# A later decay, a bonus term inside its own step, and weights prepared in the third step: another issue order for an RWKV-6 plus maxout kernel

## The chip, the cores and the metric

The kernel runs on one core of a Trainium2 chip. The metric is device time in microseconds (us) from start to end of one execution; less is better. Besides the timed runs there is one profiled execution, from which all rows below are taken. The engines are named as in the profile: PE (TensorE matmul), PEld (its weight loads), DVE (VectorE), ACT (ScalarE), POOL (GpSimd), and SPq, the queue of SyncE, which in this kernel issues every DMA.

## The reference

Two blocks follow each other. The first is a linear attention with a decaying state, for 4 batches, 8 heads, 768 tokens and a head dimension of 48:

```
state = 0
for t in range(768):
    y[t]  = r[t] @ (state + (u * k[t]) outer v[t])      # the u part is the "bonus" term
    state = w[t][:, None] * state + k[t] outer v[t]     # w is the decay, 0.8 to 0.95
```

The second is a feed-forward block on the 3072 rows of y, each of 8 x 48 = 384 numbers:

```
out = maximum(x @ w1, x @ w2) @ w_out                   # 384 -> 1024 -> 384
```

## The kernel before

**Units.** A unit is one chunk of 128 tokens of two batches; there are NU = 12, and unit n has the state g = n % 2. Inside a chunk the decay is turned into cumulative products, so that the recurrence becomes matmuls: scores inside the chunk (`scores`, `y_intra`), the part from the state (`y_inter`), and the update of the state (`kv`, `decay`). The maximum is computed as half of (sum + |difference|): |x (w1 - w2)| goes through `gate`, and x (w1 + w2) w_out / 2 through a 384 x 384 matrix `wc_sb` that `weights` prepares once: it needs the sums `ws_sb`, their 24 transpositions, 24 matmuls with `wo_sb`.

**Steps.** Step n of a software pipeline handles three units: its own unit a = n (log, cumulative sum, exponentials, scaled r and k), unit t = n - 1 (transpositions, scores, state, y) and unit m = n - 2 (feed-forward, output). There are 14 steps. The order in which every engine gets its instructions is the order of the program text (a manual schedule): an engine whose next instruction waits does nothing else, and SPq neither. So the sequence written in the main loop (L369 to L397) is the sequence on each engine.

**The decay's way.** `exps` (L203) computes the cumulative log decay `mz` of a unit. Its last row is needed on partitions, one value for each head and dimension. So it goes through DRAM: two DMAs write it to `row` (L212), two more read it back into `WL` (L216), which waits on SPq until the first have landed. `decay_exp` (L238, on ACT) makes `Wt` out of it one step later, `decay` (L264, on POOL) multiplies the state with it.

**The bonus.** `bonus_mul` (L171, POOL) casts v to bf16 (`vb`) and forms r * k * u (`rku`, two multiplications); `bonus_sum` (L181) sums it on DVE (`dg`) and multiplies v with that on POOL (`vd`). In step n they are issued for unit n + 1.

**DMAs.** On SPq a step holds, in this order: the 8 loads of unit n + 2, `row` of unit n, `WL` of unit n, and the two outputs of unit n - 2 (192 KB each, L363). An output's tile `osb` is one of three.

**PSUM.** The tag "tr" (transpositions) has one buffer, "go" (gates, outputs, wc) two, "y" one, "sc" one.

Of the kernel before, what the change touches and what calls it, by code (L numbers as in the profile page):

```python
# [8 lines left out]
F32 = mybir.dt.float32  # L9
# [25 lines left out]
def _body(tc, r, k, v, w, u, moe_w1, moe_w2, moe_w_out, out):  # L35
    nc = tc.nc
    B, H, S, D = r.shape
    P = 128
# [3 lines left out]
    HD = H * D  # L42
# [5 lines left out]
    NU = NC * B // 2  # L48
# [9 lines left out]
    def wt_(shape, dt, tag, bufs=None):  # L58
        return wk.tile(shape, dt, tag=tag, name=tag, bufs=bufs)

    def pt_(shape, dt, tag, bufs=1):
        return ps.tile(shape, dt, tag=tag, name=tag, bufs=bufs)

    def unit(n):
        return n // 2, (n % 2) * 2
# [5 lines left out]
    def load(n):  # L71
        c, b0 = unit(n)
        d = {}
        for name, src in (("w", w), ("k", k), ("r", r), ("v", v)):
            t = ldp.tile([P, H, 2, D], F32, tag="l" + name, name="l" + name)
            for b in range(2):
                nc.sync.dma_start(  # L77
                    out=t[b * Q:(b + 1) * Q].rearrange("p h i d -> p h (i d)"),
                    in_=src[b0 + b, :, c * C:(c + 1) * C, :].rearrange(
                        "h (p i) d -> p h (i d)", i=2))  # L80
            d[name] = t
        L[n] = d
# [5 lines left out]
    w1f = const.tile([P, KO, d_ff], F32)  # L88
    w2f = const.tile([P, KO, d_ff], F32)
# [29 lines left out]
    for i in range(NRK):  # L119
        t = const.tile([P, 2, 2, H, DP], BF16, name=f"rkn{i}")  # L120
# [14 lines left out]
    ws_sb = const.tile([P, KO, d_ff], BF16)  # L135
# [4 lines left out]
    def weights():  # L140
        for ko in range(KO):
            nc.vector.tensor_sub(wd_sb[:, ko, :], w1f[:, ko, :], w2f[:, ko, :])
            nc.gpsimd.tensor_add(ws_sb[:, ko, :], w1f[:, ko, :], w2f[:, ko, :])  # L143
        nc.scalar.mul(wo_sb, wof, 0.5)
        for ko in range(KO):
            tp = pt_([P, FO, P], BF16, "tr")
            for fo in range(FO):
                nc.tensor.transpose(tp[:, fo, :], ws_sb[:, ko, fo * P:(fo + 1) * P], ident)  # L148
            nc.vector.tensor_copy(
                wsT_sb.rearrange("p f (k c) -> p k f c", k=KO)[:, ko, :, :], tp)  # L150
        for ko in range(KO):
            wc_p = pt_([P, HD], F32, "go", 2)
            for fo in range(FO):
                nc.tensor.matmul(wc_p, wsT_sb[:, fo, ko * P:(ko + 1) * P],
                                 wo_sb[:, fo, :], start=(fo == 0), stop=(fo == FO - 1))
            nc.scalar.copy(wc_sb[:, ko, :], wc_p)


    U = {}

    def byi(t):
        return t.rearrange("p h i d -> p i h d")

    def logw(n):
        s = U[n] = {}
        s["lw"] = lw = wt_([P, H, 2, D], F32, "lw")
        nc.scalar.activation(lw, L[n]["w"], AF.Ln)  # L167
        s["lp"] = lp = wt_([P, H, D], F32, "lp")
        nc.gpsimd.tensor_add(lp, lw[:, :, 0, :], lw[:, :, 1, :])  # L169

    def bonus_mul(n):  # L171
        s = U[n]
        s["vb"] = vb = wt_([P, H, 2, D], BF16, "vb", 3)
        nc.gpsimd.tensor_copy(vb, L[n]["v"])
        s["rku"] = rku = wt_([P, H, 2, D], F32, "rku", 1)
        nc.gpsimd.tensor_mul(rku, L[n]["r"], L[n]["k"])  # L176
        nc.gpsimd.tensor_mul(  # L177
            byi(rku), byi(rku),
            u_b.rearrange("p (h d) -> p h d", h=H).unsqueeze(1).to_broadcast([P, 2, H, D]))

    def bonus_sum(n):  # L181
        s = U[n]
        dg = wt_([P, H, 2, 1], F32, "dg")
        nc.vector.reduce_sum(dg, s["rku"], axis=AX.X)  # L184
        s["vd"] = vd = wt_([P, 2, H, D], BF16, "vd", 3)
        nc.gpsimd.tensor_mul(byi_inv(vd), L[n]["v"], dg.to_broadcast([P, H, 2, D]))  # L186

    def byi_inv(t):
        return t.rearrange("p i h d -> p h i d")
# [13 lines left out]
    def exps(n):  # L203
        s = U[n]
        mz = s["mz"]
        nc.scalar.activation(s["A"][:, 1].rearrange("p h d -> p (h d)"), mz[:, 0], AF.Exp)
        s["iA"] = iA = wt_([P, 2, H, D], F32, "iA", 1)
        nc.scalar.activation(iA.rearrange("p i h d -> p i (h d)"), mz, AF.Exp, scale=-1.0)
        row = drp.tile([2, HD], F32, tag="row", name="row")
        for b in range(2):  # L210
            e = (b + 1) * Q
            nc.sync.dma_start(out=row[b:b + 1, :], in_=mz[e - 1:e, 1, :])  # L212
        s["WL"] = wl = WL[n % 2]
        rowv = row.rearrange("b (p r d) -> r d (b p)", r=2, d=D)
        for par in range(2):
            nc.sync.dma_start(  # L216
                out=wl[par * DP:par * DP + D, :, :].rearrange("d b p -> d (b p)"),
                in_=rowv[par])

    def scale_rk(n):  # L220
        s = U[n]
        s["rkn"] = rkn = rkn_b[n % NRK]
        nc.vector.tensor_mul(rkn[:, 0, :, :, 0:D], byi(L[n]["r"]), s["A"])
        nc.vector.tensor_mul(rkn[:, 1, :, :, 0:D], byi(L[n]["k"]), s["iA"])  # L224
# [39 lines left out]
    def decay(n):  # L264
        c, b0 = unit(n)
        if c == NC - 1:
            return
        g = b0 // 2
        nc.gpsimd.tensor_mul(S_f[g], T_f[g], U[n]["Wt"].to_broadcast([P, 2, NP, D]))  # L269
        for e in range(2):  # L270
            q = slice(e * DP, (e + 1) * DP)
            nc.gpsimd.tensor_copy(S_b[g][q, :, :, e * D:(e + 1) * D], S_f[g][q])  # L272
# [52 lines left out]
    def xt(n):  # L325
        s = U[n]
        tp = pt_([P, KO, 2, P], BF16, "tr")
        for b in range(2):
            for ko in range(KO):
                nc.tensor.transpose(tp[:, ko, b, :], s["x"][:, b, ko * P:(ko + 1) * P], ident)  # L330
        s["xT"] = xT = wt_([P, KO, 2, P], BF16, "xT")
        nc.scalar.copy(xT, tp)  # L332

    def gate(n, j):
        s = U[n]
        if j == 0:
            s["gT"] = wt_([P, FO, 2, P], BF16, "gT")
        g = pt_([P, 2, 2 * P], F32, "go", 2)
        for f in range(2):
            fo = 2 * j + f  # L340
            for ko in range(KO):
                nc.tensor.matmul(g[:, f, :], wd_sb[:, ko, fo * P:(fo + 1) * P],  # L342
                                 s["xT"][:, ko].rearrange("p j t -> p (j t)"),
                                 start=(f == 0 and ko == 0), stop=(f == 1 and ko == KO - 1),
                                 skip_group_check=True)
        nc.scalar.activation(s["gT"][:, 2 * j:2 * j + 2].rearrange("p f j t -> p f (j t)"), g,  # L346
                             AF.Abs)

    def outp(n, b):
        c, b0 = unit(n)  # L350
        s = U[n]
        o = pt_([P, HD], F32, "go", 2)
        for ko in range(KO):
            nc.tensor.matmul(o, s["xT"][:, ko, b, :], wc_sb[:, ko, :],  # L354
                             start=(ko == 0), stop=False)
        for fo in range(FO):
            nc.tensor.matmul(o, s["gT"][:, fo, b, :], wo_sb[:, fo, :],  # L357
                             start=False, stop=(fo == FO - 1))
        osb = wt_([P, HD], F32, "osb", 3)
        nc.scalar.copy(osb, o)  # L360
        tok = (b0 + b) * S + c * C
        dst = out[tok:tok + C, :].rearrange("(q i) n -> i q n", i=2)
        nc.sync.dma_start(out=dst, in_=osb)  # L363


    logw(0)
    bonus_mul(0)
    bonus_sum(0)
    for n in range(NU + 2):  # L369
        a, t, m = n, n - 1, n - 2  # L370
        A, T, M = a < NU, 0 <= t < NU, 0 <= m < NU
        if n >= 1 and n + 2 < NU:
            load(n + 2)
        if n == 1:
            weights()
        if T: transp(t, 0)
        if A: cumsum(a)
        if M: gate(m, 0)
        if T: transp(t, 1)
        if A: exps(a)  # L380
        if M: gate(m, 1)
        if T: kv(t)
        if T: scores(t, 0)
        if a + 1 < NU: logw(a + 1)
        if M: gate(m, 2)
        if M: gate(m, 3)
        if T: decay_exp(t)
        if T: scores(t, 1)
        if T: y_inter(t)
        if T: decay(t)  # L390
        if a + 1 < NU: bonus_mul(a + 1)
        if A: scale_rk(a)
        if M: outp(m, 0)
        if T: y_intra(t)
        if a + 1 < NU: bonus_sum(a + 1)
        if M: outp(m, 1)
        if T: xt(t)  # L397

    ps.release()
    drp.release()  # L400
# [33 lines left out]
```

## Time and profile before

| | |
|---|---|
| median of 3 runs | 253.65 us (251.24 to 253.86) |
| profiled execution, its own time | 251.43 us |
| its span on the core | 249.6 us |
| PE busy | 154.7 us (62%) |
| POOL busy | 122.2 us (49%) |
| DVE busy | 109.4 us (44%) |
| ACT busy | 92.0 us (37%) |
| loads of one unit | 8 DMAs of 192 KB |
| outputs of one unit | 2 DMAs of 192 KB |

The span is from the first to the last instruction of the core; the own time has 1.8 us more around it. No engine is busy for much over half of the span, so the time has to be read from waits. The profile offers these views for it: a chain of work that ended last, with start and length of each piece; a list of who waited for whom; a timeline of single instructions; groups of instructions by line; and windows, which give for a stretch the busy time of each engine, the granted clock of PE (1.00 is 2.4 GHz, 0.50 is 1.2 GHz), the busy share of the 16 DMA engines and what they moved.

### The profile page before, as it was taken

What the parts mean: (1) busy time and instruction counts of PE and PEld (TensorE: products, weight loads), DVE (VectorE), ACT (ScalarE), POOL (GpSimd) and SP (SyncE); (2) the same over time, 40 slices, a digit from 0 to 9 for tenths busy, and PEclk for the clock granted to TensorE, in tenths of its full rate; (3) what the DMA queues carried; (4) which work ended last, traced back from release to release, by engine and by line L of the source; (5) the groups of instructions that cost most, each with busy time, mean ns of one, the idle gap of its engine ahead of it and who ended that gap; (6) DMA issues with size and microseconds to landing.
All of it is one profiled execution on the core that took longest, in us unless ns stands there. A gap on an engine that the chain in (4) does not pass through costs nothing.

```text
span 249.6 us, 5117 instructions
## 1 busy us (share of the span) xinstructions
PE 154.7 (62%) x2104; PEld 104.0 (42%) x2104; DVE 109.4 (44%) x132; ACT 92.0 (37%) x161; POOL 122.2 (49%) x119
## 2 busy tenths in 40 slices
PE   0200039568869696977729819919809919989820
PEld 0000025445556464645426417507507606666510
DVE  5042781667557482828416406507406605632000
ACT  3021041526445464647126125235134234534510
POOL 7378890294968868594183192192193166000000
PEclk9999999858999999999968976997986995999995
DMA  6999995969147138247148138237337311111110
GB/s 134 208 208 390 373 201 88 198 109 149 12 127 175 17 103 188 34 131 172 17 112 188 18 103 183 31 100 179 41 98 172 49 42 25 46 26 50 50 50 36
DMA packets 65463, 28.91 MB, mean 116 GB/s; under 512 B 60424, under 2 KB 64672, under 8 KB 65440
## 3 DMA queue, kind: packets, MB, share of 16 engines
q1 hardware_dynamic: 65440, 28.59, 52.2%
q8 instruction: 16, 0.26, 0.4%
q14 instruction: 7, 0.06, 0.1%
HBM read 23.83 MB, written 4.76 MB: 115 GB/s over the span
## 4 chain that ended last, share of the span: by engine, by line
DMA 27%; PE 23%; POOL 19%; issue 11%; ACT 6%; SPq 5%; DVE 5%; DVEq 0%; POOLq 0%; ACTq 0%
DMA out_dram<-osb 13%; DMA row<-mz 9%; PE go L342 7%; PE tr L231 5%; POOL rku L176 5%; POOL rku L177 4%; POOL ws_sb L143 4%; PE go L357 3%; PE ex L195 3%; POOL Sb L272 3%; DMA u_b<-in_u_dram 2%; SPq L77 2%; ACT xT L332 2%; DVE rT L236 2%; SPq L216 2%
## 5 line engine op out<-in xcount | busy, mean ns | idle before, releaser
L184 DVE TENSOR_REDUCE dg<-rku 128x16 f32<-128x768 f32 x12 | 11.4, 953 | 86.7 <-POOL rku L177 86.7
L342 PE MATMUL go<-xT,wd_sb 128*128 128x256 bf16 x288 | 41.7, 293 | 1.0 <-ACT xT L332 1.0
L231 PE MATMUL tr<-ident,rkn 128*128 128x128 bf16 x192 | 18.3, 251 | 34.9 <-ACT xT L332 27.4
L357 PE MATMUL go<-wo_sb,gT 128*128 128x384 bf16 x192 | 35.1, 326 | 0.0
L342 PEld LDWEIGHTS <-wd_sb 128*128 128x128 bf16 x288 | 29.1, 106 | 12.5 <-issue 7.0
L286 DVE TENSOR_TENSOR M<-sc,mask 128x1024 bf16<-128x1024 f32 x24 | 29.3, 1221 | 7.9 <-PE sc L283 7.9
L231 PEld LDWEIGHTS <-rkn 128*128 128x128 bf16 x192 | 15.9, 114 | 38.9 <-issue 38.0
L169 POOL TENSOR_TENSOR lp<-lw 128x384 f32<-128x384 f32 x12 | 12.4, 1037 | 39.1 <-ACT lw L167 39.1
L346 ACT ACTIVATE gT<-go 128x512 bf16<-128x512 f32 x48 | 27.7, 593 | 10.2 <-PE go L342 9.9
L360 ACT COPY osb<-go 128x384 f32<-128x384 f32 x24 | 11.4, 474 | 41.3 <-PE go L357 19.5
L357 PEld LDWEIGHTS <-gT 128*128 128x128 bf16 x192 | 18.8, 98 | 12.4
L186 POOL TENSOR_TENSOR vd<-lv,dg 128x768 bf16<-128x768 f32 x12 | 17.7, 1474 | 12.8 <-DVE dg L184 12.8
L269 POOL TENSOR_TENSOR Sf<-Tf,Wt 128x384 f32<-128x384 f32 x10 | 8.3, 828 | 29.5 <-ACT Wt L241 28.5
L176 POOL TENSOR_TENSOR rku<-lr,lk 128x768 f32<-128x768 f32 x12 | 22.3, 1855 | 0.0
L177 POOL TENSOR_TENSOR rku<-rku,u_b 128x768 f32<-128x768 f32 x12 | 21.7, 1806 | 0.9
L195 PE MATMUL ex<-lp,tri 128*128 128x384 f32 x24 | 15.5, 741 | 7.5 <-POOL lp L169 7.5
L148 PE MATMUL tr<-ident,ws_sb 128*128 128x128 bf16 x24 | 3.1, 307 | 26.8 <-POOL ws_sb L143 22.1
L272 POOL CAST Sb<-Sf 64x384 bf16<-64x384 f32 x20 | 15.5, 776 | 1.1
L354 PE MATMUL go<-wc_sb,xT 128*128 128x384 bf16 x72 | 15.7, 328 | 0.0
L199 ACT ACTIVATE A<-ex 128x384 f32<-128x384 f32 x12 | 5.9, 490 | 24.1 <-PE ex L195 24.1
L148 PEld LDWEIGHTS <-ws_sb 128*128 128x128 bf16 x24 | 2.5, 138 | 28.3 <-POOL ws_sb L143 26.6
L224 DVE TENSOR_TENSOR rkn<-lk,iA 128x768 bf16<-128x768 f32 x12 | 13.3, 1104 | 0.0
(55 smaller groups left out, 225.8 us busy)
## 6 DMA issues: line engine op xcount, KB each, us to landing
lw<-in_w_dram SPq DMA_DIRECT2D x24, 192.0 KB
lk<-in_k_dram SPq DMA_DIRECT2D x24, 192.0 KB
lr<-in_r_dram SPq DMA_DIRECT2D x24, 192.0 KB
lv<-in_v_dram SPq DMA_DIRECT2D x24, 192.0 KB
out_dram<-osb SPq DMA_DIRECT2D x24, 192.0 KB
w1f<-in_moe_w_dram SPq DMA_DIRECT2D x1, 1536.0 KB
w2f<-in_moe_w_dram SPq DMA_DIRECT2D x1, 1536.0 KB
wof<-in_moe_w_out_dram SPq DMA_DIRECT2D x1, 1536.0 KB
```

Source lines behind the costliest of these rows:

```text
L176: nc.gpsimd.tensor_mul(rku, L[n]["r"], L[n]["k"])
L177: nc.gpsimd.tensor_mul(byi(rku), byi(rku), u_b.rearrange("p (h d) -> p h d", h=H).unsqueeze(1).to_broadcast([P, 2, H, D]))
L186: nc.gpsimd.tensor_mul(byi_inv(vd), L[n]["v"], dg.to_broadcast([P, H, 2, D]))
L195: nc.tensor.matmul(ex, tri2, lp.rearrange("p h d -> p (h d)"))
L224: nc.vector.tensor_mul(rkn[:, 1, :, :, 0:D], byi(L[n]["k"]), s["iA"])
L231: nc.tensor.transpose(tp[:, p, :, i, :], s["rkn"][:, x, i, 2 * p:2 * p + 2, :].rearrange("s r d -> s (r d)"), ident)
L272: nc.gpsimd.tensor_copy(S_b[g][q, :, :, e * D:(e + 1) * D], S_f[g][q])
L286: nc.vector.tensor_mul(M.rearrange("s e p t -> s (e p) t"), sc.rearrange("s e p t -> s (e p) t"), mask[:, i].rearrange("s i q -> s (i q)") ...
L342: nc.tensor.matmul(g[:, f, :], wd_sb[:, ko, fo * P:(fo + 1) * P], s["xT"][:, ko].rearrange("p j t -> p (j t)"), start=(f == 0 and ko == 0) ...
L346: nc.scalar.activation(s["gT"][:, 2 * j:2 * j + 2].rearrange("p f j t -> p f (j t)"), g, AF.Abs)
L354: nc.tensor.matmul(o, s["xT"][:, ko, b, :], wc_sb[:, ko, :], start=(ko == 0), stop=False)
L357: nc.tensor.matmul(o, s["gT"][:, fo, b, :], wo_sb[:, fo, :], start=False, stop=(fo == FO - 1))
```

## The change

`exps` only sends `row` off; reading it back into `WL` becomes a function of its own, `decay_load`, issued for unit t = n - 1 at the very start of step n, ahead of that step's loads. `decay` of a unit moves from the middle of its own step to the start of the next one. `bonus_mul` and `bonus_sum` of unit a are issued in step a itself, after its exponentials and after its scaling. `osb` gets 6 buffers. `weights` moves from step 1 to step 2, between the work of unit 1 and the rest of the step, and its three sums move from POOL to DVE.

```
@@ weights
-            nc.gpsimd.tensor_add(ws_sb[:, ko, :], w1f[:, ko, :], w2f[:, ko, :])
+            nc.vector.tensor_add(ws_sb[:, ko, :], w1f[:, ko, :], w2f[:, ko, :])
@@ exps
             nc.sync.dma_start(out=row[b:b + 1, :], in_=mz[e - 1:e, 1, :])
+        s["row"] = row
+
+    def decay_load(n):
+        s = U[n]
+        row = s["row"]
         s["WL"] = wl = WL[n % 2]
         rowv = row.rearrange("b (p r d) -> r d (b p)", r=2, d=D)
         for par in range(2):
...
@@ outp
-        osb = wt_([P, HD], F32, "osb", 3)
+        osb = wt_([P, HD], F32, "osb", 6)
@@ main loop
-    logw(0)
-    bonus_mul(0)
-    bonus_sum(0)
-    for n in range(NU + 2):
...
-        if n == 1:
-            weights()
...
+    def step(a, t, m):
+        A, T, M = a is not None, t is not None, m is not None
+        if T and t >= 1: decay(t - 1)
         if T: transp(t, 0)
         if A: cumsum(a)
         if M: gate(m, 0)
         if T: transp(t, 1)
         if A: exps(a)
+        if A: bonus_mul(a)
         if M: gate(m, 1)
         if T: kv(t)
         if T: scores(t, 0)
-        if a + 1 < NU: logw(a + 1)
+        if A and a + 1 < NU: logw(a + 1)
         if M: gate(m, 2)
         if M: gate(m, 3)
         if T: decay_exp(t)
         if T: scores(t, 1)
         if T: y_inter(t)
-        if T: decay(t)
-        if a + 1 < NU: bonus_mul(a + 1)
         if A: scale_rk(a)
+        if A: bonus_sum(a)
         if M: outp(m, 0)
         if T: y_intra(t)
-        if a + 1 < NU: bonus_sum(a + 1)
         if M: outp(m, 1)
         if T: xt(t)
+
+    logw(0)
+    for n in range(NU + 2):
...
+        if t is not None:
+            decay_load(t)
+        if n >= 1 and n + 2 < NU:
+            load(n + 2)
+        if n == 2:
+            step(None, t, None)
+            weights()
+            step(a, None, m)
+        else:
+            step(a, t, m)
```

## Rows read from the trace of the kernel before

**Rows 1.** The page's first line.

```profile
span 249.6 us, 5117 instructions
```

**Rows 2.** Waits of SPq: who waited for what: us in total, times, longest.

```profile
SPq L216 <- DMA row<-mz: 50.5, 12, 7.2
```

**Rows 3.** The chain that ended last, two cycles: start us, length us, what.

```profile
122.16 6.57 DMA out_dram<-osb
...
141.23 6.56 DMA out_dram<-osb
```

**Rows 4.** Timeline, 134 to 143 us: start us, length us, engine, line, operation [idle before].

```profile
135.13 1.06 SPq L212 DMA_DIRECT2D row<-mz  x2
140.30 0.84 SPq L216 DMA_DIRECT2D WL<-row  x2
...
142.81 0.21 ACT L241 ACTIVATE Wt<-WL 128x8 f32<-128x8 f32 x1 [5.15 <-DMA WL<-row]
```

**Rows 5.** Windows of 1 us; the last three columns: PE clock, DMA share, GB/s.

```profile
127.00:128.00 1.00, 0.00 (x0) 0.00 (x0) 0.00 (x0) 0.00 (x0) 1.00 (x1) 0.50 0.13 49
140.00:141.00 1.00, 1.00 (x37) 0.77 (x37) 0.40 (x1) 0.00 (x0) 0.00 (x0) 1.00 0.00 0
141.00:142.00 1.00, 1.00 (x8) 0.61 (x7) 0.00 (x0) 0.00 (x0) 0.00 (x0) 1.00 0.29 2
236.00:237.00 1.00, 1.00 (x8) 0.61 (x7) 0.00 (x0) 0.00 (x0) 0.00 (x0) 1.00 0.14 51
```

**Rows 6.** Waits of the engines over the whole span.

```profile
DVE dg L184 <- POOL rku L177: 86.7, 12, 11.2
...
ACT osb L360 <- DMA out_dram<-osb: 19.4, 6, 3.9
```

**Rows 7.** Timeline of the start, 35 to 70 us.

```profile
35.44 0.68 DVE L149 COPY wsT_sb<-tr 128x1024 bf16<-128x1024 bf16 x1
...
39.76 0.84 SPq L216 DMA_DIRECT2D WL<-row  x2
...
43.95 0.61 PE L231 MATMUL tr<-ident,rkn 128*128 128x128 bf16 x8
...
49.94 1.23 DVE L286 TENSOR_TENSOR M<-sc,mask 128x1024 bf16<-128x1024 f32 x1 [0.74 <-PE sc L283]
...
51.76 0.80 ACT L323 CAST x<-y 128x768 bf16<-128x768 f32 x1 [3.15 <-PE y L318]
...
54.33 1.01 PE L231 MATMUL tr<-ident,rkn 128*128 128x128 bf16 x8 [0.89 <-ACT xT L332]
...
68.82 0.61 PE L231 MATMUL tr<-ident,rkn 128*128 128x128 bf16 x8 [0.93 <-ACT xT L332]
```

**Rows 8.** Groups by line: busy us, mean ns of one, idle before and releaser.

```profile
L286 DVE TENSOR_TENSOR M<-sc,mask 128x1024 bf16<-128x1024 f32 x24 | 29.3, 1221 | 7.9 <-PE sc L283 7.9
...
L208 ACT ACTIVATE iA<-mz 128x768 f32<-128x768 f32 x12 | 10.1, 840 | 0.0
L167 ACT ACTIVATE lw<-lw 128x768 f32<-128x768 f32 x12 | 10.0, 835 | 3.4 <-DMA lw<-in_w_dram 3.4
...
L142 DVE TENSOR_TENSOR wd_sb<-w1f,w2f 128x1024 bf16<-128x1024 f32 x3 | 8.1, 2741 | 1.1 <-DMA w2f<-in_moe_w_dram 1.1
...
L206 ACT ACTIVATE A<-mz 128x384 f32<-128x384 f32 x12 | 6.2, 520 | 14.7 <-DVE mz L200 14.7
```

**Rows 9.** The chain that ended last, from step 11 on.

```profile
206.41 1.01 PE tr L231 x8
...
220.77 0.62 PE tr L231 x8
...
232.11 1.47 PE go L342 x12
...
238.93 0.48 ACT osb L360
```

**Rows 10.** Timeline of step 11: the first output copy of the step.

```profile
217.09 0.48 ACT L360 COPY osb<-go 128x384 f32<-128x384 f32 x1 [2.32 <-PE go L357]
```

More of the change, by code (lines that the diff above doesn't have):

```diff
@@ L363, in outp @@
         nc.sync.dma_start(out=dst, in_=osb)
-    logw(0)
-    bonus_mul(0)
-    bonus_sum(0)
-    for n in range(NU + 2):
[L370 to L373, printed above, removed]
-        if n == 1:
-            weights()
+    def step(a, t, m):
+        A, T, M = a is not None, t is not None, m is not None
+        if T and t >= 1: decay(t - 1)
         if T: transp(t, 0)
@@ L389, in _body @@
         if T: y_inter(t)
-        if T: decay(t)
-        if a + 1 < NU: bonus_mul(a + 1)
         if A: scale_rk(a)
+        if A: bonus_sum(a)
         if M: outp(m, 0)
         if T: y_intra(t)
-        if a + 1 < NU: bonus_sum(a + 1)
         if M: outp(m, 1)
         if T: xt(t)
+    logw(0)
+    for n in range(NU + 2):
+        a = n if n < NU else None
+        t = n - 1 if 0 <= n - 1 < NU else None
+        m = n - 2 if 0 <= n - 2 < NU else None
+        if t is not None:
[8 more added lines that the diff above has]
+            step(a, t, m)
     ps.release()
```

## The prediction

> **What bounds the kernel now.** I read the page's first line (the span, 249.6 us [rows 1]), then the waits of SPq, then the chain, then windows of 1 us where the chain sits on DMAs.
>
> SPq, in order, spends 50.5 us in 12 waits for `row` to land before it may read `WL` back [rows 2]. The chain repeats a cycle of 141.23 - 122.16 = 19.07 us from output to output [rows 3]. SPq fills it without a gap: outputs from 122.16, loads, `row` at 135.13, a wait until 140.30, `WL` [rows 4], outputs at 141.23.
>
> What are the DMA engines doing in it? In 127 to 128, outputs alone move 49 GB/s at a share of 0.13, in the tail 51 GB/s at 0.14 [rows 5]: 0.13 x 16 is about two engines of 16. So an output of 196,608 bytes takes 196,608 / 50 GB/s = 3.93 us and a pair 7.86 us on those two. One output is 6.57 us from issue to landing [rows 3]; I split the other 2.6 us evenly: 1.3 us before the first byte, 1.3 us until the landing is seen. Loads and `row` go to the same engines behind the outputs, so `row`, tiny as it is, lands when the two slow engines have worked off everything. From output issue to `row` landed is 140.30 - 122.16 = 18.1 us; without the 1.3 at either end, 15.5 us are work. Then nothing moves (0 GB/s in 140 to 141 [rows 5]) until `WL` and the next pair start.
>
> I call the two engines the pair queue. It is busy for about 16 of 19 us, and the missing 3 us are the round trip of `row`. The compute engines follow it: ACT waits 19.4 us for outputs to free `osb` [rows 6], and `Wt` idles 5.15 us for `WL` [rows 4]. Ahead of that, DVE waits 86.7 us for `rku` from POOL [rows 6]. That wait heads the list, but in the cycle it is covered by the longer DMA wait.
>
> **Part by part.**
>
> *Decay read back a step later.* No work is removed. On SPq, `WL` of unit n moves behind the outputs of step n and ahead of the loads of step n + 1. It still waits for `row`, but now a pair of outputs is queued between them: while the round trip runs, the pair queue has 7.86 us of outputs to do. The gap closes. A cycle is then the work alone: 15.5 us plus `WL` (0.29 of all engines in its first 1 us window [rows 5], so 0.3 to 0.5 us), **15.9 us**. The bounds: 15.2 us if the latencies I subtracted are half a microsecond longer and `WL` shorter, 19.07 us if nothing closes.
>
> *Decay applied later.* Three POOL instructions change place; they meet inputs a step old, and their result is used a step after. Nothing: the state of unit n is needed by unit n + 2. Without that cover it is their own duration, a few microseconds once.
>
> *Bonus in its own step.* Same instructions; DVE's `dg` now stands at the end of a step behind its other work, and `rku` has been made meanwhile. The 86.7 us of waiting goes; what is late next is `Wt` behind `WL`, the pair queue. So in the cycle this is worth nothing; it only lets step length fall from the 14.36 us of step 11 (220.77 - 206.41 [rows 9], PE-bound) or hold it.
>
> *Six osb buffers.* ACT's 19.4 us of waits for outputs go, with the same next wait.
>
> *Weights.* Here something is lost. The first `WL` is issued at 39.76 [rows 7], since `row` of unit 0 stands behind the first three units' loads and the weights on SPq. That stays. Before, the weights were made in the shadow of that wait; now unit 1 comes first and its ACT work stands behind `Wt` of unit 0. Counted out:
> - `WL` 39.76 + 0.84, landed and read 1.67 us later (142.81 - 141.14 [rows 4]), `Wt` 0.2: 42.5.
> - From the copy to x to the next step's first transposition 54.33 - 51.76 = 2.57 us [rows 7]: 45.1.
> - From a step's first transposition to the end of its second mask 49.94 + 1.23 - 43.95 = 7.2 us [rows 7]: 52.3. DVE starts on the weights.
> - Six sums of 1024 numbers. The differences took 2.74 us each beside POOL's sums; the mask, a DVE product of the same size, 1.22 us [rows 8]. POOL has finished unit 2's bonus by then (its inputs are in SBUF before 42) and waits for ACT's log. I take 6 x 1.22 = 7.3 us, bound 6 x 2.74 = 16.4 us: 59.6.
> - From the first `wsT` copy to the next step's first PE instruction 43.95 - 35.44 = 8.5 us [rows 7]: 68.1.
> - The rest of step 2 is feed-forward plus unit 2's exponentials. The last step, feed-forward alone, takes 238.93 - 232.11 = 6.8 us [rows 9]; on ACT its gates now share with 0.84 + 0.84 + 2 x 0.52 = 2.7 us [rows 8] (the first half-size exponential is taken like the second): 9.5, so 77.6.
>
> Step 3 thus starts at 77.6, where it started at 68.82 [rows 7]: **8.8 us lost**. And the pair queue, which has no work between unit 4's loads and the first output, gets that output later too: the pair is copied at about 76.3 and 78.1, runs from 77.6 to 85.5, and `WL` of unit 2 is through at 85.9.
>
> The Trainium skill (GPSIMD Engine Reference, Specifications) says that POOL's access to SBUF is shared with VectorE and contended by DVE instructions with two SBUF inputs. By it the 2.74 us is a price of POOL running beside, and the sum takes the lower value, as above; were the rule wrong here, the span would be 9.1 us longer.
>
> **The sum.** Seven more cycles bring `WL` of unit 9 through the queue: 85.9 + 7 x 15.9 = 197.2, seen at 198.5. How late may it be in its step? In step 11 ACT idled 2.32 us before the output copy at 217.09 [rows 10], 10.7 us into a step of 14.36; that step's first transpositions ran at 1.01 us instead of 0.62 [rows 9], so with a faster start I take 9.3 us. Step 10 starts at 198.5 - 9.3 = 189.2. Loads have ended, so steps 10 and 11 go at compute's pace: between 12.8 (step 11 with its start at the full clock, an estimate) and 14.36, say 13.5 each: step 12 at 216.2. From there the old kernel needed 249.6 - 220.77 = 28.8 us, the last of it an output queue running behind; I take 28.0 for outputs that are not late. Span **244.2**, 5.4 us less than 249.6 (8.8 lost at the start, some 14 won in the cycles and the tail).
>
> The own time of the profiled execution is 251.43, so 246.0 after; the median of the three runs is 0.9% above it, which carries over: 246.0 x 253.65 / 251.43 = 248.2. I say **248**.
>
> **The rivals.**
> 1. *The weights block costs more than the cycles give back (slower).* Place: DVE in step 2. Price: 2.74 instead of 1.22 us a sum, 9.1 us, all of it passed on, since the first outputs and everything in the queue stand behind. Slower than now as soon as the block is over 5.4 us dearer than counted, that is above 2.1 us a sum. Time 248.2 + 9.2 = 257.4. For it: the only direct row is 2.74. Against: POOL has nothing to do then.
> 2. *The gap does not close (slower).* The outputs may not be there when the loads are through: then SPq still waits for `row` with an empty pair queue. Cycle 19.07: 7 x 3.2 = 22 us more, 270. It needs outputs copied later than about 15 us into a step; I find them at 9.5 to 12.
> 3. *Compute sets the pace.* The Trainium skill (DMA: Bandwidth & Descriptors, Rules for kernel authors) advises to issue a DMA early and to wait late, and says that the fixed setup cost then overlaps. If the wait were only such a cost, it would vanish altogether. Then steps 3 to 9 take 13.5 us: 7 x 2.4 = 17 us less, a span of 227 and a time of 231. Against: in rows 5 the transfer is slow because of two engines, and 12 pairs of 7.86 us from 77.6 on end no earlier than 172 even with no loads between; with loads and `WL` (7 x 8.0) 228.
> 4. *It evens out.* The start loses 2 to 3 us more than counted, or the cycle is 16.3: 251 to 256.
>
> **How the numbers follow.** Forecast (241 to 251): 0.55. Rival 1: 0.12, rival 2: 0.06, rival 3 or an earlier start (228 to 241): 0.12, rival 4: 0.15. A measurement tells about 1% here (the three runs lie within that). Faster by over 1% is below 251.1: forecast and rival 3, 0.65 after rounding; within 1%: 0.17; slower 0.18. The range for 8 in 10 goes from 239 (cycle at 15.2, 7 x 0.7 = 5 us, and a start 4 us earlier) to 258 (rival 1).
>
> **What would show it.** Right: `Wt` waits for `WL` near 42; six DVE sums near 1.2 us from about 52; step 3 starting 7 to 10 us later than before; output pairs 15 to 16.5 us apart from then on; no window of 0 GB/s in the middle; nobody waiting for `osb`. Wrong: sums of over 2 us, step 3 after 83, pairs still 19 us apart or already 13.5.

## The result, and the profile after

The changed kernel takes 239.12 us (median of 4 runs, 237.25 to 240.01), against 253.26 us (251.24 to 253.86) of the kernel before in the same set: a ratio of 0.9445, with a 95% interval of 0.9367 to 0.9524. Ratios and intervals, here and below, go by the fast runs alone: a run over 1.5% above the fastest of its kernel is left out. The forecast was 248, some 2% faster, the range 239 to 258. So the direction was right, and the gain of 14.1 us is 2.7 times the forecast 5.3. The profiled execution took 237.25 us, its span is 8.7 us under the 244.2 of the sum.

The page's first line, the answer to [rows 1]:

```profile
span 235.5 us, 5089 instructions
```

The waits of SPq (us in total, times, longest), against the 50.5 us of [rows 2]:

```profile
SPq L368 <- ACT osb L365: 34.0, 10, 7.0
SPq L221 <- DMA row<-mz: 20.2, 9, 4.0
```

The waits for `row` are less than half. The waits for outputs that compute has not made yet lie at the start and in the tail (5.6 us up to 84, 28.4 us from 184 on); in the cycles between, SPq never waits for `osb` and waits 14.2 us in 7 pieces for `row`. The waits of the engines, against [rows 6]:

```profile
DVE rT L241 <- PE tr L236: 65.5, 11, 17.0
ACT Wt L246 <- DMA WL<-row: 60.7, 12, 9.9
...
DVE dg L184 <- POOL rku L177: 3.6, 1, 3.6
```

The 86.7 us that DVE waited for `rku` are 3.6 us, and ACT no longer waits for outputs to free `osb`. The waiting has moved: `Wt` waits for `WL` in all 12 steps that have one, 60.7 us in place of 27.7 (6 times), and DVE now waits for the transpositions that stand behind it (`rT`).

The timeline of the start (start us, length us), the answer to [rows 7]:

```profile
38.76 0.84 SPq L221 DMA_DIRECT2D WL<-row  x2
...
41.22 0.21 ACT L246 ACTIVATE Wt<-WL 128x8 f32<-128x8 f32 x1 [4.93 <-DMA WL<-row]
...
43.88 1.01 PE L236 MATMUL tr<-ident,rkn 128*128 128x128 bf16 x8 [0.89 <-ACT xT L337]
...
51.27 1.22 DVE L142 TENSOR_TENSOR wd_sb<-w1f,w2f 128x1024 bf16<-128x1024 f32 x1
...
58.08 0.69 DVE L149 COPY wsT_sb<-tr 128x1024 bf16<-128x1024 bf16 x1
...
66.51 0.81 PE L195 MATMUL ex<-lp,tri 128*128 128x384 f32 x2
...
74.08 2.32 SPq L368 DMA_DIRECT2D out_dram<-osb  x2
...
75.17 0.61 PE L236 MATMUL tr<-ident,rkn 128*128 128x128 bf16 x8
```

Each line is a term of the start's sum: step 3 begins at 75.17 where it began at 68.82, and the first output goes off at 74.08. Then the cycle, two of SPq's output pairs, with four others between them:

```profile
104.12 1.74 SPq L368 DMA_DIRECT2D out_dram<-osb  x2
...
179.28 1.93 SPq L368 DMA_DIRECT2D out_dram<-osb  x2
```

That is (179.28 - 104.12) / 5 = 15.0 us from pair to pair in place of 19.07 [rows 3] (119.49, 134.26, 149.04 and 164.30 lie between). The chain of one such cycle, against [rows 3, 4]:

```profile
118.68 0.42 SPq L212
119.15 3.65 DMA row<-mz
123.26 7.43 DMA WL<-row
131.00 0.37 ACT osb L365
...
145.90 1.49 POOL vd L186
...
148.24 0.42 SPq L212
```

`row` still takes some 4 us to land, but `WL` is issued behind the outputs and takes 7.4 us where it took under 2.6: it stands in the queue behind an output pair. The transfers never rest now: from 78 to 190 us no window of 1 us falls below 41 GB/s, and outputs alone move some 50 [rows 5]. The chain itself reads as a loop over two cycles (29.6 us from `row` at 118.68 to `row` at 148.24): 11.1 us of `row` and `WL`, then compute up to `vd`, then a load that waited for `vd` to free its buffer. Two bounds thus compete, the queue and this loop. The loop meets one output pair in two cycles, so a second pair would cost it half its price in a cycle; experiment 9 measures the whole price.

### The profile page after: what moved, and what is told of

Its sections match the earlier page's. It is cut to its first block, busy times and chain, and to the rows that moved or that the text cites. A ratio compares the mean times of both kernels' runs of the same rounds, so it can differ in the third digit from the quotient of the medians.

```text
span 235.5 us, 5089 instructions
## 1 busy us (share of the span) xinstructions
PE 157.3 (67%) x2104; PEld 105.8 (45%) x2104; DVE 106.7 (45%) x135; ACT 91.2 (39%) x161; POOL 105.7 (45%) x116
## 4 chain that ended last, share of the span: by engine, by line
PE 28%; DMA 21%; SPq 18%; DVE 12%; ACT 7%; issue 6%; POOL 3%; DVEq 0%; ACTq 0%
SPq L77 15%; DMA WL<-row 13%; DMA row<-mz 8%; PE go L347 6%; PE go L362 4%; PE tr L236 4%; PE ex L195 3%; ACT xT L337 2%; DVE M L291 2%; POOL vd L186 2%; PE go L154 2%; PE sc L288 2%; PE go L359 2%; DVE rkn L228 2%; PE tr L335 2%
## 5 line engine op out<-in xcount | busy, mean ns | idle before, releaser
L347 PE MATMUL go<-xT,wd_sb 128*128 128x256 bf16 x288 | 41.0, 290 | 2.0 <-ACT xT L337 0.9
L241 DVE COPY rT<-tr 128x1024 bf16<-128x1024 bf16 x12 | 8.3, 691 | 65.5 <-PE tr L236 65.5
L347 PEld LDWEIGHTS <-wd_sb 128*128 128x128 bf16 x288 | 28.8, 104 | 12.7 <-issue 7.1
L291 DVE TENSOR_TENSOR M<-sc,mask 128x1024 bf16<-128x1024 f32 x24 | 29.4, 1223 | 8.6 <-PE sc L288 8.6
L335 PE MATMUL tr<-ident,x 128*128 128x128 bf16 x72 | 7.3, 251 | 32.3 <-ACT x L328 32.3
L236 PE MATMUL tr<-ident,rkn 128*128 128x128 bf16 x192 | 19.3, 261 | 12.5 <-ACT xT L337 8.9
L246 ACT ACTIVATE Wt<-WL 128x8 f32<-128x8 f32 x12 | 2.5, 209 | 60.7 <-DMA WL<-row 60.7
L236 PEld LDWEIGHTS <-rkn 128*128 128x128 bf16 x192 | 16.6, 119 | 16.8 <-issue 12.0
L195 PE MATMUL ex<-lp,tri 128*128 128x384 f32 x24 | 14.8, 709 | 12.2 <-POOL lp L169 12.2
L335 PEld LDWEIGHTS <-x 128*128 128x128 bf16 x72 | 5.1, 111 | 35.9 <-ACT x L328 35.6
L167 ACT ACTIVATE lw<-lw 128x768 f32<-128x768 f32 x12 | 10.0, 837 | 19.3 <-DMA lw<-in_w_dram 19.3
L200 DVE TENSOR_TENSOR mz<-ex,lw 128x384 f32<-128x384 f32 x12 | 6.7, 558 | 19.5 <-ACT A L199 19.5
```

The costliest lines, as they stand in the source:

```text
L195: nc.tensor.matmul(ex, tri2, lp.rearrange("p h d -> p (h d)"))
L236: nc.tensor.transpose(tp[:, p, :, i, :], s["rkn"][:, x, i, 2 * p:2 * p + 2, :].rearrange("s r d -> s (r d)"), ident)
L291: nc.vector.tensor_mul(M.rearrange("s e p t -> s (e p) t"), sc.rearrange("s e p t -> s (e p) t"), mask[:, i].rearrange("s i q -> s (i q)") ...
```

## The experiments

All times are medians against the kernel before on the same chip; the changed kernel's own 239.12 is the other mark. The kernel before has medians from 252.48 to 253.72 in these sets, so a difference of 1 us between two sets tells nothing. Two theories stood against each other at first. *Pair queue*: the two DMA engines that carry outputs set the pace, and the change filled the hole in their work. *Bonus*: the gain is the 86.7 us of waits that left DVE.

**1. Read back at once** (x1): the changed kernel, `decay_load(n)` called directly behind the `row` DMAs, not at the head of the next step.

```
         s["row"] = row
+        decay_load(n)
...
-        if t is not None:
-            decay_load(t)
```

> The changed kernel with one part undone: WL is read back directly behind row again, everything else as changed. Pair-queue theory (outputs and loads share two slow DMA engines, and the change won by giving them an output pair to do during the round trip of row): the cycle goes from 15.1 back to about 19 us, eight cycles, so 28 to 31 us more than the changed kernel, about 267 us, and 1 us windows of 0 GB/s come back. Rival (the gain is the bonus term leaving DVE's path, the read-back is only moved): at most 3 us more, about 241.

Measured: 262.35 us, ratio 1.0355 (1.029 to 1.0419). Its output pairs in SPq's timeline, and a window (the last columns: PE clock, DMA share, GB/s):

```profile
133.59 1.24 SPq L369 DMA_DIRECT2D out_dram<-osb  x2
...
152.38 1.25 SPq L369 DMA_DIRECT2D out_dram<-osb  x2
```

```profile
151.00:152.00 1.00, 1.00 (x35) 0.83 (x34) 0.00 (x0) 0.00 (x0) 0.38 (x1) 0.82 0.00 0
```

The pairs are 18.8 us apart again and the windows of 0 GB/s are back. That is 23 us lost, 5 to 8 less than the theory expected. With this one part undone, the rest of the change makes the kernel 9 us slower than it was. The bonus theory falls here.

**2. Bonus for unit a + 1 again** (x2): the changed kernel, `bonus_mul(a + 1)` behind `y_inter` and `bonus_sum(a + 1)` behind `y_intra`, as before.

```
-        if A: bonus_mul(a)
...
         if T: y_inter(t)
+        if A and a + 1 < NU: bonus_mul(a + 1)
...
-        if A: bonus_sum(a)
...
         if T: y_intra(t)
+        if A and a + 1 < NU: bonus_sum(a + 1)
```

> The changed kernel with the bonus term issued for unit a + 1 again, at its old places. Pair-queue theory: DVE's long waits for rku come back but the cycle stays at 15 us: 237 to 242. Rival (the bonus made the gain): most of the 14 us are lost again, 248 to 252.

Measured: 239.91 us, ratio 0.9449 (0.9371 to 0.9526), the changed kernel's time. The bonus order is worth nothing here. DVE's long waits for `rku` were expected back and do not come back in the cycles:

```profile
DVE dg L184 <- POOL rku L177: 32.1, 4, 11.1
```

All four lie ahead of 84 us. So in the cycles it was not the bonus order that took these waits away (see experiment 5).

**3. Weights at the head of step 1** (x3): the changed kernel with `if n == 1: weights()` ahead of `step(a, t, m)`, and step 2 in one piece.

> The changed kernel with the weights prepared at the head of step 1 as before, the sums on DVE. Pair-queue theory: the weights lie in the shadow of the wait for the first WL, the first output pair is issued at 62 to 66 us in place of 74.1 and everything behind it moves along: 8 to 10 us less, 229 to 231. Rival (the start is hidden behind later waits, or step 1 becomes as much longer as step 2 gets shorter): 237 to 241.

Measured: 228.79 us, ratio 0.9021 (0.8945 to 0.9097), 10.3 us less than the changed kernel; the first output pair goes out at 62.84 us. Moving the weights behind unit 1 is a loss: the pair goes out 11.2 us sooner, and nearly all of that reaches the end.

**4. Outputs in two halves** (x4): the changed kernel, each output as two DMAs of 64 rows.

```
-        nc.sync.dma_start(out=dst, in_=osb)
+        for i in range(2):
+            nc.sync.dma_start(out=dst[i], in_=osb[i * Q:(i + 1) * Q, :])
```

> The changed kernel with each output sent as two DMAs of 64 rows, one for each parity, in place of one DMA over both. Pair-queue theory: if such a DMA is spread over all 16 engines, an output takes well under 1 us, the tail windows show far above 50 GB/s, the cycle falls from 15.1 to the 12.9 to 13.5 us of the compute engines, and the last output lands 4 to 6 us sooner: 235.5 - 8 x 1.8 - 5 = 216 span, 217 to 222 us. Rival (the loads or the engines set the 15.1 us, outputs are only in line): the cycle stays, only the end is sooner, 232 to 236.

Measured: 209.73 us, ratio 0.8269 (0.8206 to 0.8333), better than expected. In its windows the tail's outputs run at

```profile
205.00:206.00 1.00, 0.00 (x0) 0.00 (x0) 0.00 (x0) 0.00 (x0) 0.00 (x0) 1.00 0.44 105
...
206.20:206.40 0.20, 0.00 (x0) 0.00 (x0) 0.00 (x0) 0.00 (x0) 0.00 (x0) 1.00 1.02 230
```

where they ran at some 50 GB/s and a share of 0.13 to 0.14 [rows 5]. The second line, 0.2 us long, shows all 16 engines at work. And its `Wt` no longer waits:

```profile
107.07 0.21 ACT L246 ACTIVATE Wt<-WL 128x8 f32<-128x8 f32 x1
119.13 0.21 ACT L246 ACTIVATE Wt<-WL 128x8 f32<-128x8 f32 x1
```

The cycle is 12.06 us: that is compute's pace, and the chain holds no transfer from 95 to 180 us. The same bytes in another shape no longer show in the cycle; so the limit was the two engines. Compute's pace itself came out below the 12.9 to 13.5 us expected. One thing differs beside the waits: PE's mean granted clock is 0.997, in the changed kernel 0.933 (last section). How much of the step that is worth was not tried by itself. The Trainium skill (DMA: Bandwidth & Descriptors, Why a DMA increments its semaphore by 16 and not by 1) explains the shape: the number of engines is the largest up to 16 that divides the slowest dimension of both sides. An output view led by a parity of 2 gets two, one of 64 rows sixteen; the runs agree with it (shares of 0.13 and 1.02).

**5. Read-back, with six buffers** (x5): the kernel before, with `decay_load(t)` at the head of step n and six `osb` buffers; decay, bonus and weights as they were.

> The kernel before with one part of the change alone: WL is read back at the head of the next step, and osb has six buffers; decay, bonus and weights stay where they were. Pair-queue theory: the cycle falls from 19.1 to 15.1 us as in the changed kernel, but step 3 still starts at 69 and the first pair goes out at 66, so it beats the whole change: 235.5 - 8 = 226 to 231 us. Rival (the later decay and the bonus are needed too, since POOL's chain from Wt over decay and rku to dg holds the next step's transpositions): the cycle stays at 17 us or more, 240 to 250.

Measured: 236.0 us, ratio 0.9331 (0.9251 to 0.941). These two parts, of which the buffers alone bring nothing (experiment 6), bring no less than the whole change (236.0 against 239.12, with intervals that overlap). I had expected more (226 to 231). Its `Wt` in the timeline of ACT:

```profile
94.60 0.21 ACT L246 ACTIVATE Wt<-WL 128x8 f32<-128x8 f32 x1 [2.27 <-DMA WL<-row]
...
185.02 0.21 ACT L246 ACTIVATE Wt<-WL 128x8 f32<-128x8 f32 x1 [1.06 <-DMA WL<-row]
199.57 0.20 ACT L246 ACTIVATE Wt<-WL 128x8 f32<-128x8 f32 x1
214.09 0.21 ACT L246 ACTIVATE Wt<-WL 128x8 f32<-128x8 f32 x1 [2.90 <-DMA WL<-row]
```

The first two are 6 cycles apart: 15.07 us each, the queue's pace, and at 185.02 it leads the changed kernel (191.12, below) by 6 us. Then loads end, and its next two steps take 14.55 and 14.52 us, where the changed kernel takes 11.5 and 12.7. So the theory and its rival were both partly right: the cycle is the queue's alone, and the rest of the order pays where compute sets the pace. Which part of the rest? DVE's waits for `rku` are still there:

```profile
DVE dg L184 <- POOL rku L177: 70.0, 12, 11.3
```

From 84 to 186 us they are 39.4 us in 7 pieces, and none in experiment 2. The two kernels differ in the place of the decay and in the weights, which are made before 84 us. So it is the later decay that takes these waits away.

**6. Six osb buffers alone** (x6): the kernel before with `"osb", 6`.

> The kernel before with six osb buffers and nothing else. Pair-queue theory: the 19.4 us of waits for an output's landing turn into waits for WL, the cycle stays at 19 us: 250 to 255, no difference to before. Rival (the output buffers made the gain): 235 to 242.

Measured: 253.48 us, ratio 1.0014 (0.9954 to 1.0073). No difference. The 19.4 us of waits for `osb` only covered other waits, though not `WL` as expected: `Wt` waits 24.5 us for it, against 27.7 before.

**7. Sums on POOL** (x7): the changed kernel with `nc.gpsimd.tensor_add(ws_sb...)`.

> The changed kernel with the three sums of the weights on POOL again, still in step 2. If POOL running beside DVE is what made a sum of 1024 numbers take 2.74 us, DVE's three differences take 2.7 us again and POOL's sums 3.3, in parallel from about 48 us on: the first wsT copy at 59 to 60 in place of 58.1, and 238 to 242 us, no difference to the changed kernel. Rival 1 of the prediction turned round (DVE's six operations are what the start waits for): the three sums off DVE bring 3 us, 235 to 236.

Measured: 239.51 us, ratio 0.9488 (0.942 to 0.9556): no difference in time. In the views of its two lines (durations in ns, least/median/most; first and last start):

```profile
L142 DVE TENSOR_TENSOR wd_sb<-w1f,w2f x3: 1211/2823/2823, 52.7 to 58.2; 128x1024 bf16<-128x1024 f32 x3
```

```profile
L143 POOL TENSOR_TENSOR ws_sb<-w1f,w2f x3: 2347/2351/2353, 44.9 to 49.5; 128x1024 bf16<-128x1024 f32 x3
```

and POOL's bonus work (its timeline):

```profile
52.59 1.81 POOL L176 TENSOR_TENSOR rku<-lr,lk 128x768 f32<-128x768 f32 x1
54.48 2.67 POOL L177 TENSOR_TENSOR rku<-rku,u_b 128x768 f32<-128x768 f32 x1
```

POOL, with DVE not on the weights, takes 2.35 us a sum, where it took 3.3 us beside DVE. DVE's first two differences take 2.82 us each (52.7 to 58.2), beside POOL's bonus work; the third, with POOL done at 57.15, takes 1.21. The same instruction has two prices. The ends alternate (POOL 54.40, DVE 55.48, POOL 57.15, DVE 58.2), as if the two took turns; that is a reading of this one stretch.

**8. Both that helped** (x8): experiments 3 and 4 together.

> The changed kernel with both edits that helped: outputs in two DMAs of 64 rows, and the weights at the head of step 1. If the start and the cycle are separate costs, the gains add: 209.7 - 10 = 198 to 203 us. Rival (without the slow queue the start is hidden by something else, the loads above all): 206 to 210.

Measured: 200.56 us, ratio 0.7919 (0.786 to 0.7978). The two gains add (29.4 us, then 9.2, where the second alone brought 10.3): start and cycle are separate costs. It beats both kernels, and by far.

**9. Outputs twice** (x9, one execution): the changed kernel, each `osb` sent a second time, into a scratch tensor in DRAM.

```
         nc.sync.dma_start(out=dst, in_=osb)
+        scr = drp.tile([C, HD], F32, tag="scr", name="scr", bufs=8)
+        nc.sync.dma_start(out=scr.rearrange("(q i) n -> i q n", i=2), in_=osb)
```

> The changed kernel with every output sent a second time, into a scratch tensor in DRAM: twice the suspected load. It measures the price of a pair in the cycle. Pair-queue theory with 50 GB/s on two engines: the cycle grows by 7.9 us from 15.1 to 23.0 us; seven cycles and a tail that is then bound by outputs give a span near 305 to 315. Rival (outputs run on 16 engines at some 200 GB/s): 2 us a cycle, a span near 252. The rest of the cycle, loads, row and WL, is what is left after the measured price of the pair: I expect 7.2 us in place of the 8.0 of the prediction.

Measured: a span of 328.8 us. `Wt` of units 2 and 9:

```profile
93.23 0.21 ACT L246 ACTIVATE Wt<-WL 128x8 f32<-128x8 f32 x1 [11.75 <-DMA WL<-row]
...
253.97 0.21 ACT L246 ACTIVATE Wt<-WL 128x8 f32<-128x8 f32 x1 [11.99 <-DMA WL<-row]
```

(253.97 - 93.23) / 7 = 22.96 us a cycle, 7.81 more than the changed kernel's 15.15 (below): the price of a pair, and 7.86 was expected. I had forgotten one pair ahead of unit 2's `WL` and half of the tail, so the span came out beyond my 315. What remains of the cycle for loads, `row` and `WL` is 15.15 - 7.81 = 7.34 us.

**10. Read back at once, outputs in halves** (x10): experiments 1 and 4 together.

> Outputs in two DMAs of 64 rows, and WL read back directly behind row as in the kernel before: is the later read-back worth anything without the slow pair in the queue? Theory (the round trip cost what it did because it left the slow queue empty, and now there is no slow queue): SPq waits 3 to 4 us for row in a cycle, and its own issues (8 loads, row, WL, 4 outputs) fill 10 to 11 us, so the cycle is 13 to 14 us in place of 12.06: 217 to 224 us. Rival (any wait for the round trip on SPq is on the path in full): the cycle is 16, about 240. Second rival (it is hidden altogether): 208 to 211.

Measured: 215.22 us (213.2 to 219.06), ratio 0.8463 (0.8366 to 0.8561). That is below the 217 to 224 the theory expected and above the 208 to 211 of the second rival. By the ratios (0.8463 against 0.8269 in experiment 4) the later read-back is worth some 4.9 us without the slow pair, not 23.

**11. The kernel before with its outputs in halves** (x11): nothing else.

> The kernel before with the outputs in two DMAs of 64 rows and nothing else. Theory: the cycle of 19.1 us falls to the 13.7 us that the steps took at the start of the kernel before, where DVE waited for rku; step 3 still starts at 69: span 212 to 217, 214 to 219 us. Rival (the order of issue is needed as well): over 228.

Measured: 217.35 us, ratio 0.8627 (0.8531 to 0.8724), as expected; `Wt` comes every 13.71 us. One edit to the shape of a DMA gains 36 us, the whole reordering 14.

**12. Bonus for unit a + 1, outputs in halves** (x13): experiments 2 and 4 together.

> Outputs in two DMAs of 64 rows, and the bonus term for unit a + 1 at its old places, the later decay kept: what is the bonus order worth once the slow queue is gone and compute sets the pace? Theory (its cover was the queue): POOL reaches rku only after lp, some 7 us into a step, and takes 4.5 us for it, dg 1 us more, and the next step's transpositions wait: a cycle of 12.6 to 13.7 us in place of 12.06, eight cycles: 214 to 222 us. Rival (it is worth nothing at any pace): 208 to 211.

Measured: 210.61 us, ratio 0.8364 (0.8297 to 0.843): the theory is wrong here and the rival right. The bonus order is worth nothing at compute's pace either; POOL is through with `rku` in time. What separates the 13.71 us steps of the old order (experiment 11) from 12.06 is then most likely the decay within its own step, behind `Wt` and ahead of `rku` on POOL. The chain of experiment 11 goes round just there, at a granted clock of 1.00 and with no wait for `WL`:

```profile
117.92 0.22 ACT Wt L241
118.21 0.61 POOL Sf L269
...
122.41 1.81 POOL rku L176
...
127.00 0.69 DVE rT L236
```

That the decay's place removes the waits for `rku` is shown (experiments 2 and 5). That it alone is worth the 1.65 us a step is argued: experiments 11 and 13 also differ in read-back, buffers and weights, and no run moved the decay alone.

## Why the prediction was right and wrong, point by point

`Wt` of the changed kernel, units 2, 8, 9, 10 (timeline of ACT):

```profile
85.06 0.21 ACT L246 ACTIVATE Wt<-WL 128x8 f32<-128x8 f32 x1 [3.87 <-DMA WL<-row]
...
176.03 0.21 ACT L246 ACTIVATE Wt<-WL 128x8 f32<-128x8 f32 x1 [3.87 <-DMA WL<-row]
191.12 0.21 ACT L246 ACTIVATE Wt<-WL 128x8 f32<-128x8 f32 x1 [6.35 <-DMA WL<-row]
202.59 0.21 ACT L246 ACTIVATE Wt<-WL 128x8 f32<-128x8 f32 x1 [1.45 <-DMA WL<-row]
```

and the chain from step 11 on, against [rows 9]:

```profile
193.85 1.01 PE tr L236 x8
...
207.19 0.62 PE tr L236 x8
```

| term of the sum | forecast | measured | the span is off by |
|---|---|---|---|
| `WL` of unit 2 seen (start and first pair) | 87.2 | 85.06 | -2.1 |
| seven cycles | 7 x 15.9 | 106.06 = 7 x 15.15 | -5.2 |
| from `WL` of unit 9 to the start of step 11 | 13.5 - 9.3 = 4.2 | 2.73 | -1.5 |
| step 11 | 13.5 | 13.34 | -0.2 |
| step 12 to the end | 28.0 | 28.3 | +0.3 |

The sum is -8.7, from 244.2 to 235.5.

**The mechanism held.** The pair queue is the bound (x4, x9), the hole in it was the round trip of `row` (x1), the reordered read-back closes it (x5), the bonus order is worth nothing (x2, x13), nor are six buffers in the old order (x6; with the later read-back they were not tried apart), and the weights block loses at the start (x3). There I counted 8.8 us lost at step 3; it was 75.17 - 68.82 = 6.35 us. Its terms were 42.5, 52.3, 59.6, 68.1 and 77.6; measured were 41.43, 51.27, 58.08, 66.51 and 75.17. None was off by more than 1.1 us of its own, and all but one (late by 0.04) came early. One cause was named wrong: the prediction let the 86.7 us of waits for `rku` go by the bonus order and put the later decay at nothing. In the cycles the waits went by the decay (x2, x5); the bonus order took only those of the start. While the queue sets the cycle, that changes no time.

**The step that failed is the size of the cycle**: "without the 1.3 at either end, 15.5 us are work". That made a cycle of 15.9 us with `WL`, with a lower bound of 15.2; it was 15.15, and seven of them are 5.2 of the 8.7 us. The pair was right (7.81 measured, 7.86 forecast); the rest was 7.34 instead of 8.0. The windows of the kernel before, behind an output issue at 141.23, show what I had taken for work:

```profile
142.00:143.00 1.00, 0.46 (x3) 0.07 (x1) 0.00 (x0) 0.19 (x2) 0.00 (x0) 1.00 0.23 13
143.00:144.00 1.00, 0.00 (x0) 0.00 (x0) 0.00 (x0) 1.00 (x3) 0.84 (x2) 1.00 0.15 37
144.00:145.00 1.00, 0.51 (x6) 0.39 (x7) 0.00 (x0) 0.08 (x1) 0.96 (x2) 1.00 0.10 29
```

Outputs that start on an empty queue come slowly: 13 + 37 + 29 = 79 KB in 3 us. At 50 GB/s from 142.5 on it would be 125 KB; the missing 46 KB are 0.9 us. It is not only `WL` that is in the way: the pair of 204.06 in the changed kernel's tail, with no `WL` ahead of it still under way, starts no faster on an empty queue:

```profile
206.00:207.00 1.00, 0.25 (x5) 0.13 (x3) 0.00 (x0) 1.00 (x2) 0.28 (x1) 1.00 0.14 32
```

In the cycles of the changed kernel the outputs follow the loads and run at once:

```profile
122.00:123.00 1.00, 0.92 (x22) 0.77 (x23) 0.99 (x3) 1.00 (x3) 1.00 (x1) 1.00 0.14 48
123.00:124.00 1.00, 1.00 (x21) 0.73 (x22) 0.78 (x1) 1.00 (x3) 0.75 (x2) 1.00 0.17 51
```

So the hole was not the 3.2 us of a silent queue but 3.9 (19.07 - 15.15), slow start included. This is arithmetic on windows; no run changed the start of the outputs alone, and why they start slowly is open.

**A slip of the joining**: I let `WL` come 9.3 us into a step and then gave the step its own 13.5 us. In a cycle longer than compute's step, `Wt` is what ends the step: it came 12.4 us in (191.12 - 178.76, the step's first transposition), and after it only two output copies, x, its transposition and xT remain, 2.73 us.

**The rivals.** The first had the wrong place: POOL was idle, and the sums took 1.22 us. Its price of 2.74 us was a mean of unlike ones: in the kernel before the three differences took 1.50, 3.36 and 3.37 us, the long ones beside POOL's sums, and beside POOL's bonus work they take 2.82 (x7). As the Trainium skill has it (GPSIMD Engine Reference, Specifications), POOL's access is contended by DVE instructions with two SBUF inputs; x7 agrees, with 2.82 us beside POOL and 1.21 after it. The second did not occur: no window without traffic in the cycles. The third, and the advice of the Trainium skill beside it (DMA: Bandwidth & Descriptors, Rules for kernel authors), came true only with the queue gone (x4): the trip of `row` could then be overlapped, and its place in the order is worth some 4.9 us (x10). The time itself lies in the bin of the third rival and an earlier start (228 to 241, chance 0.12), mostly for another reason, the shorter cycle.

## What to carry to other kernels

Where a DMA wait heads the chain, ask first how many DMA engines the transfer in front of it uses: share times 16, from one window. Two engines at 50 GB/s were worth 36 us by an edit of two lines (x11), more than twice what a reordering around them brought. A part that is worth nothing under a slow queue is priced only when the queue is gone: test it at compute's pace before keeping or dropping it. And a move that helps can hide one that hurts: here the later read-back with its buffers gains 17 us, the weights' new place loses 10.

## What the hardware showed that I had not expected

- A load issue on SPq takes 0.64 us when the queue is free and over 2 us behind an output pair (4.39 us for the two w loads at 123.45 in the timeline of the kernel before). Meanwhile the windows from 126 to 128 show two of 16 engines at work (share 0.13 to 0.14), so the other fourteen stand idle. An output pair is not the only thing that does it: behind the weights' loads, at 16.87 in the changed kernel, the two w loads take 8.66 us.
- An instruction's price depends on its neighbour: a DVE sum or difference of 1024 numbers takes 1.21 us alone, 2.82 beside POOL's products (x7) and 3.36 beside POOL's sums (kernel before); POOL's sum takes 2.35 or 3.33 us.
- The way of 3 KB (two DMAs) into DRAM, with nothing in the queue, is short: in experiment 11, in the last steps, `WL` is issued 1.5 us behind `row` (183.50 to 184.96). Of the 5.2 us that this takes in the cycle before (135.13 to 140.30), the larger part was the queue in front of it.
- A wait of PE can cost clock. In the changed kernel PE stands idle from 130 to 132, behind the wait of `Wt`; in the window after that its granted clock is 0.55, then 0.50 (1.2 GHz) until 138:

```profile
135.00:136.00 1.00, 1.00 (x2) 0.24 (x2) 0.58 (x1) 0.00 (x0) 0.92 (x2) 0.50 1.31 210
```

Eight transpositions take 1.01 us there in place of 0.61. PE is busy in all windows from 134 on, and from 139 the clock is 1.00 again. In experiment 4, where `Wt` does not wait, the mean granted clock is 0.997.
